# Writing the zero rows of an expert layer's output later, and issuing weight loads behind the first gathers

## The chip, the cores and the metric

The kernel runs on one core of one Trainium2 chip. The metric is the device time of one execution in microseconds (us), lower is better. Three runs of the kernel before gave 581.94, 584.55 and 584.72 us; the median is 584.55 us.

## What is computed

A global filter layer (real FFT along the sequence, product with a complex filter, inverse FFT) feeds an expert layer with a capacity: of the tokens whose largest logit belongs to an expert, only the 80 with the largest gate weight go through it. All other rows of the output are zero.

```python
X = np.fft.rfft(x, axis=1)                       # x: 8 x 2496 x 256, float32
y = np.fft.irfft(X * (filt_r + 1j * filt_i), n=2496, axis=1).reshape(19968, 256)
logits = y @ w_gate                              # 8 experts
expert_idx = np.argmax(logits, axis=1)
gate_w = softmax(logits)[row, expert_idx]
out = np.zeros((19968, 256), np.float32)
for e in range(8):
    tok_idx = the 80 rows of expert e with the largest gate_w
    out[tok_idx] = gate_w[tok_idx, None] * (np.maximum(y[tok_idx] @ w1[e], 0) @ w2[e])
```

So 19,968 rows of 1 KB are written as zero, and 8 x 80 of them are overwritten by the expert outputs.

## The kernel before

The transform of 2496 = 39 x 64 points is done as two matrix products with tables, one batch element (of 8) after another. A loop of steps k = 10 b + u, ten for each batch element b, interleaves three kinds of TensorE work:

- `stage2(b, u)`, line 347, multiplies two frequency blocks by the table `d_t`; VectorE multiplies by the filter (line 354) and GpSimd combines (lines 359, 361).
- `stage1(b + 1, u)`, line 289, in steps u = 0 to 5, transforms one of six chunks of the next batch element's input `x`; ScalarE copies the product and issues its write to a buffer `d1` in device memory (line 292).
- `turn(b, u)`, line 371, two steps later, turns the filtered spectrum and computes gate terms. For batch elements 3 to 6 the spectrum goes to device memory as `yf` (line 399); for 0, 1, 2 and 7 it stays on the chip.

Transfers of the loop: `load_x` (line 267, tile `x`, three transfers a chunk) reads input three steps ahead; `load_t2` (line 298, tile `t`, ten transfers for a batch element) reads the turned `d1` back in steps 7, 8 and 9. Both are issued by SP in the order of the program: an SP instruction that waits holds up all that follow on SP. Each SP or ScalarE transfer takes one of eight completion semaphores, and where one is taken again the earlier transfer on it is waited for, so some eight transfers are under way at a time.

`put_zeros(n)` (lines 182 to 190) issues the next n of 26 zero writes, each 768 rows (786,432 bytes) from one tile of zeros. It is called with 1 after every third step from k = 11 on (line 546), and with all that are left (`NZ`) at line 816.

After the loop come the last two batch elements' gate terms (lines 409 to 507), the token pick (`pick`, lines 594 to 753: a long chain of small VectorE operations), and `back` (lines 763 to 792) for each batch element: a gather of table rows for the picked tokens by GpSimd (line 772, tile `gt`), transposes (line 781) and products with the spectrum (line 786). `spectrum` (line 796, tile `yb`) reads `yf` back for batch elements 3 to 6; the first two reads are issued ahead of the pick. Then a branch (line 822), not taken here, and the experts: `gather(e)` (line 851, tile `xg`) takes an expert's 80 rows, `layer1` (lines 861 to 874) and `layer2` (lines 882 to 886) compute, `load_weights` (lines 581, 583, tile `w`) reads 2 MB for an expert.

Inside the loop the order is that of the program. Behind it a scheduler orders each engine's instructions, and it may place a transfer that depends on nothing ahead of where it is written.

Of the kernel before, what the change touches and what calls it, by code (L numbers as in the profile page):

```python
# [38 lines left out]
NZ = 26  # L39
# [36 lines left out]
def kernel(  # L76
# [107 lines left out]
    def put_zeros(n):  # L184
        for i in zeros[:n]:
            r = N // NZ
            m = r * C // 128
            nc.sync.dma_start(
                out=out[i * r:i * r + r, :].rearrange("r d -> (r d)").rearrange(
                    "(p k m) -> p k m", p=128, m=512),  # L190
                in_=zero_t[:].unsqueeze(1).to_broadcast([128, m // 512, 512]))
        del zeros[:n]
# [4 lines left out]
    with ExitStack() as fctx:  # L197
# [315 lines left out]
        with tc.manual_schedule():  # L513
            load_tables(0)
            load_tables(1)
            for ch in range(5):
                load_x(0, ch)
            load_d(0)
            load_x(0, 5)
            for t in range(B, B + NX):  # L520
                nc.gpsimd.dma_start(out=y_sel[128 * t:128 * t + 128, :], in_=zero_t[:, 0:C])
            xs = [(b, ch) for b in range(1, B) for ch in range(len(CHUNKS))]

            def ahead(g):
                if g < NS // SG:
                    if g:
                        load_d(g)
                    for k in range(2):
                        load_filter(k, g)

            def step(k):
                b, u = divmod(k, NU)
                if b < B:
                    stage2(b, u)
                if b + 1 < B and u < len(CHUNKS):

                    while xs and xs[0] <= divmod(6 * b + 6 + u + min(k, 3), 6):
                        load_x(*xs.pop(0))
                    stage1(b + 1, u)
                if k >= LATE:  # L540
                    turn(*divmod(k - LATE, NU))
                if b + 1 < B and u in (7, 8, 9):
                    for g in ((0, 1), (2, 3), (4,))[u - 7]:
                        load_t2(b + 1, g)
                if k % 3 == 2 and k >= NU:
                    put_zeros(1)
                if b % 2 == 0 and 0 < b < B and u in (2, 3, 5, 6, 8):
                    logits(b // 2 - 1, (2, 3, 5, 6, 8).index(u))
                if b % 2 == 1 and 1 < b < B and u in (1, 2, 4, 5, 7, 9):
                    gating(b // 2 - 1, (1, 2, 4, 5, 7, 9).index(u))  # L550

            ahead(0)
            ahead(1)
            for ch in range(len(CHUNKS)):
                stage1_near(ch)
            for g in range(NS // SG):
                turn_near(g)
                for k in range(2):
                    turn_filter(k, g)
                ahead(g + 2)  # L560
                step(2 * g)
                step(2 * g + 1)
                if g == NS // SG - 1:
                    load_tables(2)
            for k in range(NU, B * NU + LATE):
                step(k)
            for part in range(5):
                logits(B // 2 - 1, part)
            for part in range(NG):
                gating(B // 2 - 1, part)  # L570
# [185 lines left out]
    def gather_gates():  # L756
        nc.gpsimd.memset(gate[:], 0.0)
        for e in range(E):
            nc.gpsimd.indirect_dma_start(
                out=gate[:, e:e + 1], out_offset=None, in_=gates_dram[:, :],  # L760
                in_offset=bass.IndirectOffsetOnAxis(ap=idxs[:, e:e + 1], axis=0),
                bounds_check=N - 1, oob_is_err=False)

    def back(mp, mps, nm, loads, put, idx, start=True, stop=True, acc=None, pad=False):


        gt = mp.tile([128, NS * 128], F32, name=f"gt_{nm}", tag="gt")
        kw = {}
        if pad:
            nc.gpsimd.memset(gt[:], 0.0)  # L770
            kw = dict(bounds_check=S - 1, oob_is_err=False)
        nc.gpsimd.indirect_dma_start(
            out=gt[:], out_offset=None, in_=rows[:, :],
            in_offset=bass.IndirectOffsetOnAxis(ap=idx, axis=0), **kw)
        yb = loads()
        wt = mp.tile([128, NS, 128], F32, name=f"wt_{nm}", tag="wt")
        for g in range(NS // SG):
            ps = mps.tile([128, SG, 128], F32, name=f"pw_{nm}_{g}", tag="pt")
            for i in range(SG):
                s = SG * g + i  # L780
                nc.tensor.transpose(ps[:, i, :], gt[:, 128 * s:128 * s + 128], ident[:])  # L781
            copy = nc.vector.tensor_copy if g % 2 == 0 else nc.scalar.copy
            copy(out=wt[:, SG * g:SG * g + SG, :], in_=ps[:])  # L783
        po = mps.tile([128, C], F32, name=f"pr_{nm}", tag="po") if acc is None else acc
        for s in range(NS):
            nc.tensor.matmul(po[:], lhsT=wt[:, s, :], rhs=yb[s // SG][:, s % SG, :],  # L786
                             start=(start and s == 0), stop=(stop and s == NS - 1))
        if put is not None:
            yr = mp.tile([128, C], F32, name=f"yr_{nm}", tag="yr")
            nc.vector.tensor_copy(out=yr[:], in_=po[:])  # L790
            nc.sync.dma_start(out=y_sel[put:put + 128, :], in_=yr[:])
        return po

    def spectrum(pool, tag, b, nm):
        yb = pool.tile([128, NS, C], F32, name=f"yb_{nm}", tag=tag)
        nc.sync.dma_start(out=yb, in_=yf[b])
        return [yb[:, SG * g:SG * g + SG, :] for g in range(NS // SG)]

    away = [b for b in range(B) if b not in KEEP]
    with (  # L800
        tc.tile_pool(name="mp", bufs=2) as mp,
        tc.tile_pool(name="mps", bufs=2, space=PSUM) as mps,
    ):
        yb = {b: spectrum(keep_b, "kb", b, f"{b}") for b in away[:2]}
        with (
            tc.tile_pool(name="pick", bufs=1) as sp,
            tc.tile_pool(name="pkps", bufs=1, space=PSUM) as pp,
        ):
            pick(sp, pp)
        for i, b in enumerate(away):  # L810
            back(mp, mps, f"{b}", lambda: yb.pop(b), 128 * b, idxb[:, b:b + 1])
            if i + 2 < len(away):
                yb[away[i + 2]] = spectrum(keep_b, "kb", away[i + 2], f"{away[i + 2]}")
            else:
                load_weights(i + 2 - len(away))
        put_zeros(NZ)
        for b in KEEP:
            back(mp, mps, f"{b}", lambda: yk[b], 128 * b, idxb[:, b:b + 1])
        gather_gates()

    n_bad = nc.values_load(bad[0:1, 0:1], min_val=0, max_val=1 << 20)
# [56 lines left out]
    def layer2(e):  # L878
# [10 lines left out]
            in_=ys[:], in_offset=None, bounds_check=N - 1, oob_is_err=False,  # L889
        )  # L890

    for e in range(2, 5):
        load_weights(e)
    gather(0)
    gather(1)
    layer1(0)
    for e in range(E):
        if e + 2 < E:
# [392 lines left out]
```

## Time and profile before

| | |
|---|---|
| median of 3 runs | 584.55 us |
| profiled execution | 586.85 us |
| its span on the core | 585.0 us |
| PE (TensorE matmul) busy | 464.3 us (79%) |
| DVE, ACT, POOL busy | 222.2, 127.0, 174.5 us |
| moved by DMA | 135.92 MB, 232 GB/s over the span |
| waits of line 289 for `x`, whole span | 26.2 us |
| waits of line 347 for `t`, whole span | 17.7 us |

PE is TensorE's matmuls, PEld its weight loads, DVE is VectorE, ACT ScalarE, POOL GpSimd, SP SyncE. The clock column gives the TensorE clock that was granted, as a share of full speed: 0.50 is 1.2 GHz and 1.00 is 2.4 GHz. The DMA share is the mean busy share of the core's 16 DMA engines; the profile shows stretches a little over 1.00. The profiled execution's 586.85 us is its span and 1.85 us around it.

### The profile page before, as it was taken

To read this page: it belongs to the slowest core of one execution; us is meant where nothing else is said; L and a number is where in the kernel's file an instruction comes from. 1 tells how busy PE (TensorE), PEld (TensorE's weight loads), DVE (VectorE), ACT (ScalarE), POOL (GpSimd) and SP (SyncE) were. 2 spreads that over 40 slices of the span, in tenths; PEclk is the share of its full clock that TensorE was granted. 3 is DMA by queue.
4 is the path that set the end of the run, shared out by engine and by line. 5 is a ranking of instruction groups with operands and counts; after the bars stand their busy time and mean duration, and the time that the engine had idled before them with its cause. 6 is when DMAs were issued, how large, how long until landed. Compare 5 with 4: busy or idle time off the path is not lost. (4 is left out here: it accounts for less than half of the span.)

```text
span 585.0 us, 7928 instructions
## 1 busy us (share of the span) xinstructions
PE 464.3 (79%) x2867; PEld 380.5 (65%) x2867; DVE 222.2 (38%) x500; ACT 127.0 (22%) x236; POOL 174.5 (30%) x253
## 2 busy tenths in 40 slices
PE   6498979789877989894997887114999999199994
PEld 6466948578656758574676874013888888098882
DVE  5334724335537316553325853781112211000110
ACT  2124323323332323431331221000001100000110
POOL 5012423414327324445334560115200100202111
PEclk9879988899979879997989995555999999659997
DMA  7968997978989989999998921704798620676700
GB/s 215 222 183 230 252 321 254 271 258 267 291 281 303 344 302 281 359 292 299 332 310 235 354 78 57 302 1 180 259 360 275 247 99 12 222 250 214 257 12 11
DMA packets 63625, 135.92 MB, mean 232 GB/s; under 512 B 6652, under 2 KB 35324, under 8 KB 61916
## 3 DMA queue, kind: packets, MB, share of 16 engines
q1 hardware_dynamic: 51956, 93.46, 51.9%
q0 software_dynamic: 5824, 22.90, 10.5%
q10 hardware_dynamic: 5800, 18.98, 9.9%
q8 instruction: 25, 0.41, 0.3%
q14 instruction: 20, 0.16, 0.1%
HBM read 83.16 MB, written 52.16 MB: 231 GB/s over the span
## 5 line engine op out<-in xcount | busy, mean ns | idle before, releaser
L354 DVE TENSOR_TENSOR p<-pb,ft 128x512 f32<-128x512 f32 x160 | 102.7, 683 | 50.0 <-PE pb L347 38.5
L359 POOL TENSOR_TENSOR yt<-p,p 128x256 f32<-128x256 f32 x80 | 59.7, 746 | 188.4 <-DVE p L354 143.9
L371 PEld LDWEIGHTS py<-gi,yt 128*128 128x128 f32 x640 | 88.1, 200 | 33.3 <-issue 22.4
L289 PE MATMUL pa<-x,wf_t 117*120 117x512 f32 x154 | 86.5, 686 | 26.2 <-DMA x<-in_x_dram 26.2
L347 PE MATMUL pb<-d_t,t 128*128 128x128 f32 x640 | 89.8, 285 | 17.7 <-DMA t<-d 17.7
L371 PE MATMUL py<-gi,yt 128*128 128x136 f32 x640 | 92.8, 290 | 8.6 <-POOL yt L361 8.6
L347 PEld LDWEIGHTS pb<-d_t,t 128*128 128x128 f32 x640 | 81.7, 199 | 21.2 <-issue 20.8
L291 ACT COPY t<-pa 120x512 f32<-120x512 f32 x77 | 44.5, 586 | 122.1 <-PE pa L289 99.1
L289 PEld LDWEIGHTS pa<-x,wf_t 117*120 117x120 f32 x154 | 28.6, 208 | 49.3 <-issue 44.8
L394 DVE TENSOR_REDUCE z<-py 128x16 f32<-128x32 f32 x80 | 15.2, 189 | 116.9 <-ACT ysp L391 66.3
L361 POOL TENSOR_TENSOR yt<-p,p 128x256 f32<-128x256 f32 x80 | 59.2, 740 | 0.0
L868 PEld LDWEIGHTS ph<-xs,w 128*128 128x128 f32 x256 | 36.1, 227 | 0.6
L786 PE MATMUL pr<-yb,wt 128*128 128x256 f32 x160 | 36.3, 382 | 0.0
L868 PE MATMUL ph<-xs,w 128*128 128x80 f32 x256 | 36.0, 311 | 0.0
L786 PE MATMUL pr<-yk,wt 128*128 128x256 f32 x160 | 35.9, 379 | 0.0
L391 ACT COPY ysp<-py 128x512 f32<-128x512 f32 x40 | 23.2, 585 | 49.5 <-PE py L371 42.6
L781 PE MATMUL pw<-ident,gt 128*128 128x128 f32 x160 | 24.3, 296 | 11.1 <-DMA gt<-rows_tbl,idxb 8.3
L783 ACT COPY wt<-pw 128x512 f32<-128x512 f32 x16 | 9.4, 586 | 107.4 <-PE pw L781 107.4
L786 PEld LDWEIGHTS pr<-yb,wt 128*128 128x128 f32 x160 | 30.1, 192 | 3.7
L391 ACT COPY yk<-py 128x512 f32<-128x512 f32 x40 | 23.3, 585 | 41.7 <-PE py L371 40.0
L786 PEld LDWEIGHTS pr<-yk,wt 128*128 128x128 f32 x160 | 29.8, 190 | 3.7
L882 PE MATMUL po<-w,hT 128*80 128x256 f32 x128 | 31.0, 392 | 0.0
(157 smaller groups left out, 377.9 us busy)
## 6 DMA issues: line engine op xcount, KB each, us to landing
out_dram<-zero_t SPq DMA_DIRECT2D x26, 768.0 KB
x<-in_x_dram SPq DMA_DIRECT2D x120, 156.0 KB
t<-d SPq DMA_DIRECT2D x70, 256.0 KB
d<-t ACTq DMA_DIRECT2D x35, 480.0 KB
w<-in_moe_w_dram SPq DMA_DIRECT2D x16, 1024.0 KB
yf<-ysp POOLq DMA_DIRECT2D x20, 512.0 KB, 7.1
yb<-yf SPq DMA_DIRECT2D x4, 2560.0 KB
x<-in_x_dram SPq DMA_DIRECT2D x23, 78.0 KB
```

What stands on the lines that cost most here:

```text
L289: nc.tensor.matmul(out=ps[0:NM1], lhsT=wf_t, rhs=xt[0:NP1, 2 * i:2 * i + 2, :], start=True, stop=True)
L291: nc.scalar.copy(out=t1[:, 2 * i:2 * i + 2, :], in_=ps[0:NM1])
L347: nc.tensor.matmul(out=ps[:, i, cb], rhs=d_t[:, s, :], start=True, stop=True, lhsT=st["t2", b, s // SG][:, s % SG, 128 * cb:128 * cb + 128])
L354: nc.vector.tensor_tensor(out=pt, in0=ps[:].rearrange("p s c r q -> p (s c) r q"), in1=f.unsqueeze(2).to_broadcast([128, 2 * NDB, 2, NQ]), ...
L359: nc.gpsimd.tensor_tensor(out=yt[:, :, 0, :], in0=pr[0][:, :, 0, :], in1=pr[1][:, :, 1, :], op=AL.subtract)
L361: nc.gpsimd.tensor_tensor(out=yt[:, :, 1, :], in0=pr[0][:, :, 1, :], in1=pr[1][:, :, 0, :], op=AL.add)
L371: nc.tensor.matmul(out=ps[:, i, 136 * cb:136 * cb + 136], rhs=gi[:, cb, :], lhsT=yt[:, 2 * i + cb].rearrange("p r q -> p (r q)"), start=Tr ...
L391: nc.scalar.copy(out=ys[:, m:m + 2, :].rearrange("p i (k c) -> p i k c", k=NDB), in_=ps[:, :, 0:288].rearrange("p i (k c) -> p i k c", k=N ...
L781: nc.tensor.transpose(ps[:, i, :], gt[:, 128 * s:128 * s + 128], ident[:])
L786: nc.tensor.matmul(po[:], lhsT=wt[:, s, :], rhs=yb[s // SG][:, s % SG, :], start=(start and s == 0), stop=(stop and s == NS - 1))
L868: nc.tensor.matmul(ph[:, fc // 4, fc % 4, 0:cap], lhsT=w1s[e][:, k, 128 * fc:128 * fc + 128], rhs=xs[:, k, :], start=(k == 0), stop=(k == ...
L882: nc.tensor.matmul(po[0:cap, :], lhsT=hT[:, fc, :], rhs=w2s[e][:, fc, :], start=(fc == 0), stop=(fc == NFC - 1))
```

## The change

The call in the loop is gone. Ten zero writes are written in the program ahead of the first two spectrum reads, six behind them, and then 4, 4 and 2 behind the `back` of batch elements 0, 1 and 2. At the experts, the loads of the weights 2 to 4 are written behind `gather(0)` and `gather(1)`.

```diff
@@ step(k), in the loop
-                if k % 3 == 2 and k >= NU:
-                    put_zeros(1)
@@ behind the loop
+        put_zeros(10)
         yb = {b: spectrum(keep_b, "kb", b, f"{b}") for b in away[:2]}
+        put_zeros(6)
...
-        put_zeros(NZ)
         for b in KEEP:
             back(mp, mps, f"{b}", lambda: yk[b], 128 * b, idxb[:, b:b + 1])
+            put_zeros(4 if b < 2 else 2)
         gather_gates()
@@ experts
+    gather(0)
+    gather(1)
     for e in range(2, 5):
         load_weights(e)
-    gather(0)
-    gather(1)
     layer1(0)
```

On SP, in the loop around the reads `t` of batch element 3, the kernel before has these rows (`x` and `t` are the loads, `out_dram<-zero_t` a zero write; the number in `t_3_0` is the batch element, then the group):

```order
L267 DMA x_0_1177<-in_x_dram 39x1024 x3
L188 DMA out_dram<-zero_t 384x1x512
L267 DMA x_1_1221<-in_x_dram 39x1024 x3
L267 DMA x_2_1252<-in_x_dram 39x1024 x3
L188 DMA out_dram<-zero_t 384x1x512
L298 DMA t_3_0_1333<-d_3_1073 64x4x256 x2
L298 DMA t_3_1_1336<-d_3_1073 64x4x256 x2
L298 DMA t_3_2_1358<-d_3_1073 64x4x256 x2
L298 DMA t_3_3_1361<-d_3_1073 64x4x256 x2
L298 DMA t_3_4_1394<-d_3_1073 64x4x256 x2
L188 DMA out_dram<-zero_t 384x1x512
L267 DMA x_3_1410<-in_x_dram 39x1024 x3
```

And the changed kernel at the same place:

```order
L267 DMA x_0_1173<-in_x_dram 39x1024 x3
L267 DMA x_1_1216<-in_x_dram 39x1024 x3
L267 DMA x_2_1247<-in_x_dram 39x1024 x3
L298 DMA t_3_0_1327<-d_3_1070 64x4x256 x2
L298 DMA t_3_1_1330<-d_3_1070 64x4x256 x2
L298 DMA t_3_2_1352<-d_3_1070 64x4x256 x2
L298 DMA t_3_3_1355<-d_3_1070 64x4x256 x2
L298 DMA t_3_4_1388<-d_3_1070 64x4x256 x2
L267 DMA x_3_1403<-in_x_dram 39x1024 x3
```

Seventeen single zero writes have left SP's queue between the loads of batch elements 1 and 7 in this way.

On SP from the last input chunk of the loop to the fourth spectrum read, before (`yb` is a spectrum read, `y_sel` the result rows of a `back`):

```order
L267 DMA x_5_2465<-in_x_dram 1x512
L188 DMA out_dram<-zero_t 384x1x512 x4
L298 DMA t_7_0_2659<-d_7_2404 64x4x256 x2
...
L298 DMA t_7_3_2688<-d_7_2404 64x4x256 x2
L188 DMA out_dram<-zero_t 384x1x512
L298 DMA t_7_4_2723<-d_7_2404 64x4x256 x2
L188 DMA out_dram<-zero_t 384x1x512 x4
L796 DMA yb_3096<-yf_122 128x5120
L796 DMA yb_3098<-yf_123 128x5120
L821 TENSOR_LOAD bad
```

And in the changed kernel:

```order
L267 DMA x_5_2448<-in_x_dram 1x512
L188 DMA out_dram<-zero_t 384x1x512 x4
L298 DMA t_7_0_2640<-d_7_2387 64x4x256 x2
...
L298 DMA t_7_4_2703<-d_7_2387 64x4x256 x2
L188 DMA out_dram<-zero_t 384x1x512 x8
L794 DMA yb_3082<-yf_122 128x5120
L794 DMA yb_3084<-yf_123 128x5120
L188 DMA out_dram<-zero_t 384x1x512 x13
L794 DMA yb_3297<-yf_124 128x5120
L789 DMA y_sel<-yr_3294 128x256
L188 DMA out_dram<-zero_t 384x1x512
```

Four zero writes stand ahead of the last batch element's `t` reads in both; eight now follow them where five stood, thirteen follow the first two spectrum reads, and one stands behind the third.

On SP behind the branch the kernel before loads the weights in these rows:

```order
L822 UNCONDITIONAL_BRANCH x2
L581 DMA w_7094<-in_moe_w_dram 128x2x1024
L583 DMA w_7094<-in_moe_w_dram 128x8x256
L581 DMA w_7097<-in_moe_w_dram 128x2x1024
L583 DMA w_7097<-in_moe_w_dram 128x8x256
```

And the changed kernel in these:

```order
L822 UNCONDITIONAL_BRANCH x2
L579 DMA w_7098<-in_moe_w_dram 128x2x1024
L581 DMA w_7098<-in_moe_w_dram 128x8x256
L579 DMA w_7101<-in_moe_w_dram 128x2x1024
L581 DMA w_7101<-in_moe_w_dram 128x8x256
```

Only line numbers and names differ. The gathers are issued by GpSimd, another queue, whose rows behind the branch are also the same in both kernels, and so are the semaphores that the loads and the gathers wait for.

## Rows read from the trace of the kernel before

**Rows 1.** Windows: span, busy us of PE, PEld, DVE, ACT, POOL, clock, DMA share, GB/s.

```profile
85.00:295.00 210.00, 179.33 (x1086) 139.58 (x1087) 93.30 (x191) 67.12 (x118) 85.59 (x125) 0.91 0.94 295
345.00:403.00 58.00, 20.19 (x133) 14.79 (x132) 31.22 (x107) 4.53 (x9) 11.10 (x16) 0.55 0.31 120
```

**Rows 2.** Groups of PE's instructions from 85 to 295 us: busy, mean | idle before.

```profile
L289 PE MATMUL pa<-x,wf_t 117*120 117x512 f32 x114 | 65.3, 698 | 17.0 <-DMA x<-in_x_dram 17.0
...
L347 PE MATMUL pb<-d_t,t 128*128 128x128 f32 x400 | 55.6, 284 | 13.7 <-DMA t<-d 13.7
```

**Rows 3.** Windows around the first wait for x in the loop.

```profile
81.00:84.00 3.00, 0.00 (x0) 0.00 (x0) 0.19 (x2) 1.66 (x3) 0.00 (x0) 1.00 0.88 299
...
87.00:90.00 3.00, 3.00 (x10) 1.95 (x9) 0.00 (x0) 1.09 (x2) 0.00 (x0) 0.50 0.93 328
```

**Rows 4.** Timeline of PE: start, us, instruction, count, idle before and what ended it.

```profile
73.35 1.88 PE L289 MATMUL pa<-x,wf_t 117*120 117x512 f32 x4
...
84.85 3.74 PE L289 MATMUL pa<-x,wf_t 117*120 117x512 f32 x4 [4.26 <-DMA x<-in_x_dram]
...
188.65 1.13 PE L347 MATMUL pb<-d_t,t 128*128 128x128 f32 x8 [2.25 <-DMA t<-d]
...
207.66 3.74 PE L289 MATMUL pa<-x,wf_t 117*120 117x512 f32 x4 [3.34 <-DMA x<-in_x_dram]
```

**Rows 5.** Timeline of SP's queue: zero writes and the loads beside them.

```profile
84.44 1.08 SPq L188 DMA_DIRECT2D out_dram<-zero_t  x1
...
179.91 0.54 SPq L188 DMA_DIRECT2D out_dram<-zero_t  x1
...
188.81 0.62 SPq L188 DMA_DIRECT2D out_dram<-zero_t  x1
...
195.83 9.64 SPq L267 DMA_DIRECT2D x<-in_x_dram  x6
...
278.84 0.57 SPq L188 DMA_DIRECT2D out_dram<-zero_t  x1
...
294.80 4.48 SPq L188 DMA_DIRECT2D out_dram<-zero_t  x4
```

**Rows 6.** The page's list of DMA issues: count, KB each.

```profile
out_dram<-zero_t SPq DMA_DIRECT2D x26, 768.0 KB
...
yb<-yf SPq DMA_DIRECT2D x4, 2560.0 KB
```

**Rows 7.** Issue of the zero writes on SP: ns least, median, most; first and last.

```profile
L188 SPq DMA_DIRECT2D out_dram<-zero_t x26: 539/596/2300, 84.4 to 326.9; - x26
```

**Rows 8.** Windows of the loop's end and of the spectrum reads.

```profile
332.00:336.00 4.00, 3.85 (x34) 3.65 (x33) 3.93 (x10) 1.17 (x2) 2.79 (x4) 1.00 1.04 409
...
340.00:344.00 4.00, 3.11 (x28) 2.92 (x27) 1.93 (x6) 1.45 (x4) 3.85 (x7) 1.00 0.02 5
...
368.00:372.00 4.00, 1.08 (x4) 0.71 (x4) 2.31 (x5) 0.26 (x2) 2.02 (x4) 0.50 0.98 420
...
376.00:380.00 4.00, 0.00 (x0) 0.00 (x0) 3.73 (x13) 0.00 (x0) 0.00 (x0) 0.50 0.03 7
```

**Rows 9.** Timeline: spectrum reads, first table gather, first transposes.

```profile
362.06 0.95 SPq L796 DMA_DIRECT2D yb<-yf  x2
...
396.38 1.06 POOL L772 DMA_INDIRECT gt<-rows_tbl,idxb  x1 [3.21 <-issue]
...
403.15 3.85 PE L781 MATMUL pw<-ident,gt 128*128 128x128 f32 x16 [8.33 <-DMA gt<-rows_tbl,idxb]
```

**Rows 10.** Timeline behind the branch, and the landing time of all xg gathers.

```profile
501.61 0.39 SPq L581 DMA_DIRECT2D w<-in_moe_w_dram  x1
...
502.67 0.91 POOL L851 DMA_INDIRECT xg<-y_sel,idxg  x1 [35.02 <-DVEq L822]
...
510.27 0.50 PE L861 MATMUL px<-ident,xg 80*128 80x80 f32 x2 [12.48 <-DMA w<-in_moe_w_dram]
...
DMA to landing us min/median/max: 6.0/6.7/7.2
```

## The prediction

> **What bounds the kernel now.** I read the windows by stage first. From 85 to 295 us, the part of the loop in which single zero writes are issued, the 16 DMA engines are busy for 0.94 of the time while PE is busy for 179.33 of 210 us at a mean clock of 0.91 [rows 1]. So the transfers are the fuller of the two. The groups of PE's instructions in the same stretch say what PE waits for: 17.0 us for the input `x` and 13.7 us for the turned spectrum `t` [rows 2], 30.7 us together, and no wait for another engine is near that size. The timeline shows single waits: 4.26 us for `x` at 84.85, 2.25 us for `t` at 188.65, 3.34 us for `x` at 207.66 [rows 4]. Each has a second cost. After PE stood still from 81 to 84, the granted clock was 0.50 from 87 to 90 [rows 3], which is 1.2 GHz, and four matmul records of line 289 took 3.74 us where they take 1.88 us at 73.35 [rows 4].
>
> Over the stretch, a mean clock of 0.91 means 18% of the time at half speed: (1 - 0.91) / 0.5. That is 37.8 us, and if PE worked through it, half of it, 18.9 us, is lost. Waits and clock together are an upper bound of what better fed matmuls could give: 30.7 + 18.9 = 49.6 us. PE's own work at full clock, with its other waits, is then 210 - 49.6 = 160.4 us.
>
> Behind the loop, from 345 to 403 us, it is the other way: DMA share 0.31, and VectorE's chain of small operations sets the end [rows 1].
>
> **The change, part by part.** Part one takes zero writes out of the loop. Between 84.44 and 278.84 SP issues 17 single ones; the first and the last are shown, and each is 768 KB, 786,432 bytes [rows 5, 6]. The four issued at 294.80 [rows 5], ahead of the last `t` reads, stay where they are by the order of the changed kernel, so the delay that they cause there stays too; I cost that at nothing.
>
> What is one such write worth to the DMA engines? The window from 332 to 336, which holds mostly zero writes, moved 409 GB/s at a full share [rows 8]: 786,432 bytes / 409 GB/s = 1.92 us. Seventeen are 32.7 us. The stretch had 0.94 x 210 = 197.4 us of DMA work; 164.7 us are left. PE needs 160.4 us. The two become equally full.
>
> The gain of the loop is now bounded from both sides. Before, the stretch took 210 us with 197.4 us of the fuller resource, a factor of 1.064. Were that factor kept, it would take 164.7 x 1.064 = 175 us, a gain of 35 us. The factor should get worse, since two resources that are equally full wait for each other in turn. The low end: if only SP's issue time is won, it is 17 x 0.596 us [rows 7] = 10 us. Two observations place the value between. The wait at 84.85 came with no zero write ahead of it (the first is issued at 84.44), so a part of the waits is made by the loads' own burst: `t` and `x` together. Against that, in the batch element around 200 us the zero writes of 179.91 and 188.81 stand ahead of the `x` load of 195.83 [rows 5], whose data ended the wait at 207.66; 2 x 1.92 = 3.8 us of transfers stand against 2.25 + 3.34 = 5.6 us of waits [rows 4]. Nothing there, two thirds here: I take half of the 49.6 us, 25 us. The stretch then takes 185 us, a factor of 1.12 over 164.7.
>
> Part two is where the writes go. Eight stand behind the last `t` reads where five stood. Three more are 5.8 us. DMA fell to 5 GB/s at 340 to 344 [rows 8], and the spectrum reads start only at 362.06 [rows 9]: 22 us of idle DMA hide them. Without that cover they would delay the spectrum reads by 5.8 us, which have 403.15 - 376 = 27 us to spare: the reads are done at 376, where the rate falls to 7 GB/s [rows 8], and their first use comes after the transposes that start at 403.15 [rows 9]. Cost nothing.
>
> Thirteen stand behind the two spectrum reads, in the token pick. The two reads are 5.24 MB [rows 6], 12.5 us at 420 GB/s; thirteen zero writes are 10.22 MB, 25.0 us at 409 GB/s [rows 8]. From 362.06 this ends at 399.6 us. The first table gather is issued by GpSimd at 396.38 and its data start PE at 403.15 [rows 9]. So 3.2 us of zero writes are still under way, in the latency of the gather for the most part. PE waits on that gather, and everything behind it follows, so what it loses is on the path. The ends: 0 if the overlap falls into the latency. At the loop's 295 GB/s [rows 1] the thirteen need 34.7 us behind the reads' 376, to 410.7; if the gather has to wait for all of that, as much as 410.7 - 399.6 = 11 us. I take 2 us, near the measured rate.
>
> The Trainium skill (DMA: Bandwidth & Descriptors, Where 436 GB/s comes from) states that transfers between device memory and SBUF are held to about 358 GB/s for a core. The windows with 409 and 420 GB/s [rows 8] differ from that, and the measurement decides. By the page, an estimate, the 15.46 MB would end 43.2 us after 362.06, at 405.3, and the gather would meet 8.9 us of them. The same page (Queues, rings and completion order) states that each DMA engine takes turns between queues, so the gather would share the engines and not wait its full turn behind the zero writes. No row here shows two such queues against each other. By both rules the loss would be some 4 us instead of 2, an estimate, and the time 564 us.
>
> Nothing on VectorE's chain waits for a transfer that the change moves. Behind the thirteen on SP stand the third spectrum read, which cannot start before the first `back` ends, and the load of the branch's flag, needed only behind the last `back`. The one zero write behind the third spectrum read is 1.92 us of DMA in a stage that PE fills: nothing.
>
> Part three, weights behind the gathers, moves no instruction: rows and semaphores on SP and GpSimd are the same. SP issues the first weight load at 501.61, GpSimd the first gather at 502.67, and PE starts at 510.27 after a wait of 12.48 us [rows 10]. The gather takes 7.6 us there against a median of 6.7 us [rows 10], so even a true reordering would be worth about 0.9 us. I take 0, ends 0 and 0.9.
>
> The sum: 25 - 2 + 0 = 23 us. The profiled execution took 586.85 us, 585.0 us of it span, and would become 563.85 us. It stands 2.3 us above the median of the three runs, 584.55 us, by which the change is measured: 584.55 - 23 = 561.6, so 562 us.
>
> **The rivals.** First, the loop is bound by the burst and the order of the loads, not by bytes. For it: the wait at 84.85 with no zero write ahead, and SP issues loads in order, so `x` stands behind ten `t` reads. Against it: the share of 0.94 over the whole stretch. Then only SP's 10 us are won, less 2 us: 584.55 - 8 = 577 us.
>
> Second, nearly all waits go, and the clock stays up: the full 35 us, no loss at the gather, 584.55 - 35 = 549.6, so 550 us. For it: the zero writes account for two thirds of the waits near 200 us, and removing a wait also removes the slow stretch behind it. Against it: PE's 160.4 us and DMA's 164.7 us leave no slack.
>
> Third, on the other side: the thirteen zero writes hold the first gather until they have drained. Its place is 396 to 411 us, its price the 11 us above. It decides only from the point where the loop wins less than that. With the loop at 5 us (half of SP's issue time), the time is 584.55 + 11 - 5 = 591 us. Against it: the gather is issued on another queue than the writes.
>
> A fourth, that the change does not do what it says, is true of the weights, at 0 us, and partly of the zero writes: twelve of the 26 are placed ahead of the pick, in the loop's last batch element. That is in the sum.
>
> **How the numbers follow.** My forecast, 562 us with its own range of 554 to 572, has a chance of 0.63; the burst (577) 0.16; the full gain (550) 0.15; the held gather (591) 0.06. The range of 546 to 578 reaches over the second rival and most of the first, and leaves out the third and the tails. About 0.5% (2.9 us, 581.6 to 587.5) is what a measurement of this kernel can tell from no change. Of the first rival's 0.16, 0.06 lie there; faster: 0.63 + 0.15 + 0.10 = 0.88, same 0.06, slower 0.06.
>
> **What would show it.** In the loop, PE's waits for `x` and `t` over the same batch elements should fall from 30.7 us to about half, the mean clock rise above 0.94, and the last single-write stretch end some 25 us earlier. The distance from the spectrum reads to the first transposes should stay at 41 us (403.15 - 362.06) plus about 2, with the DMA share near 1 for some 37 us of it. From the branch to the end nothing should change. The forecast is wrong if those waits stay near 30 us, or if the transposes start 5 us or more later against the reads.

## The result, and the profile after

The changed kernel took 557.29 us, median of four runs (554.01 to 562.65), beside 584.63 us for the kernel before (581.94 to 587.22): a ratio of 0.9514, 95% interval 0.9425 to 0.9603. Measured twice more, beside the experiments, it gave 560.76 us at 0.9655 (0.9608 to 0.9703) and 558.84 us at 0.9627 (0.9575 to 0.9679). So the change is worth 20 to 28 us. The profiled executions of three experiments below (e4, e7, e9) were disturbed ones and longer than their undisturbed runs; from these three only single distances are used, never a total.

The profiled execution of the changed kernel took 554.01 us, 551.8 us of it span. The span falls into pieces at points that every trace has: first load of a turned spectrum `t`; issue of the two spectrum reads `yb`; issue of the first table gather; first transposes of what it brought; first transposes of the token gather behind the branch (`px`).

| us | before | after |
|---|---|---|
| start to first `t` | 62.38 | 61.11 |
| loop: first `t` to `yb` | 299.68 | 264.90 |
| `yb` to first gather | 34.32 | 34.33 |
| first gather to its transposes | 6.77 | 10.99 |
| transposes to `px` | 107.12 | 105.71 |
| `px` to end | 74.73 | 74.76 |

In this pair of profiles the loop gave 34.8 us, and the first gather took 4.2 us back. Little else moved: the pieces before the loop and behind the transposes are 1.3 and 1.4 us shorter.

Windows of the changed kernel (columns as in [rows 1]):

```profile
85.00:255.00 170.00, 158.21 (x1043) 126.69 (x1042) 91.61 (x187) 64.53 (x114) 81.34 (x120) 0.98 0.88 268
326.00:337.00 11.00, 1.09 (x4) 0.71 (x4) 8.26 (x15) 1.34 (x3) 2.02 (x4) 0.56 0.91 360
337.00:343.00 6.00, 1.02 (x2) 0.10 (x2) 4.58 (x19) 0.00 (x0) 0.00 (x0) 0.50 0.97 337
343.00:369.00 26.00, 2.63 (x39) 2.48 (x39) 14.82 (x62) 0.00 (x0) 9.41 (x11) 0.50 1.05 398
```

The first row answers to the first of [rows 1]: in the loop the clock is 0.98 where it was 0.91, PE is busy for 93% of the time where it was 85%, and the DMA share has fallen from 0.94 to 0.88. The other three answer to [rows 8] and to the idle stretch of [rows 1]: from the spectrum reads to the first transposes the engines are now full nearly all the time.

PE's groups from the first `t` load (61 us) to the last `t` loads (before: the stretch of [rows 2]; after: 62 to 284 us):

```profile
L347 PE MATMUL pb<-d_t,t 128*128 128x128 f32 x495 | 67.0, 279 | 3.1 <-DMA t<-d 3.1
L289 PE MATMUL pa<-x,wf_t 117*120 117x512 f32 x132 | 65.2, 613 | 10.9 <-DMA x<-in_x_dram 10.7 <-issue 0.2
```

The waits for `x` and `t` fell from 17.0 and 13.7 us [rows 2] to 10.7 and 3.1 us, and one matmul of line 289 from a mean of 698 ns to 613 ns: that is the clock.

Timeline of the changed kernel (start, us, engine, instruction, idle before):

```profile
83.43 2.24 PE L289 MATMUL pa<-x,wf_t 117*120 117x512 f32 x4 [3.79 <-DMA x<-in_x_dram]
...
104.03 1.13 PE L347 MATMUL pb<-d_t,t 128*128 128x128 f32 x8 [2.56 <-DMA t<-d]
...
264.51 5.42 SPq L188 DMA_DIRECT2D out_dram<-zero_t  x4
281.86 7.55 SPq L298 DMA_DIRECT2D t<-d  x10
289.46 14.09 SPq L188 DMA_DIRECT2D out_dram<-zero_t  x8
326.01 1.28 SPq L794 DMA_DIRECT2D yb<-yf  x2
327.36 30.64 SPq L188 DMA_DIRECT2D out_dram<-zero_t  x13
...
360.34 1.06 POOL L770 DMA_INDIRECT gt<-rows_tbl,idxb  x1 [3.21 <-issue]
...
371.33 3.85 PE L779 MATMUL pw<-ident,gt 128*128 128x128 f32 x16 [12.55 <-DMA gt<-rows_tbl,idxb]
374.97 0.66 PE L784 MATMUL pr<-yb,wt 128*128 128x256 f32 x2
...
468.85 0.39 SPq L579 DMA_DIRECT2D w<-in_moe_w_dram  x1
...
477.04 0.50 PE L861 MATMUL px<-ident,xg 80*128 80x80 f32 x2 [11.79 <-DMA xg<-y_sel,idxg]
```

The wait at 83.43, the first of the loop, is nearly that of 84.85 in [rows 4]: no zero write stood ahead of it in either kernel. The zero writes stand where the prediction put them: four ahead of the last `t` loads, eight behind, thirteen behind the spectrum reads. The gather's data now end a wait of 12.55 us where it was 8.33 us [rows 9]. From the weight load to `px` it is 8.19 us, before 8.66 us [rows 10].

One row was not foreseen. The issue of the zero writes (ns least, median, most), to be read beside [rows 7]:

```profile
L188 SPq DMA_DIRECT2D out_dram<-zero_t x26: 547/1795/9237, 264.5 to 385.3; - x26
```

Singly, a write left SP in 596 ns. In a row most take about as long as their transfer (1795 ns against 1.92 us), and one, behind the spectrum reads, took 9.24 us, so thirteen hold SP for 30.64 us. Here nothing urgent stood behind them (the third `yb` read left at 384.30 us); in experiment e7 something did.

### The profile page after: what moved, and what is told of

It is laid out like the page before. It is cut to its first block, busy times and chain, and to the rows that moved or that the text cites. A ratio compares the mean times of both kernels' runs of the same rounds, so it can differ in the third digit from the quotient of the medians.

```text
span 551.8 us, 7938 instructions
## 1 busy us (share of the span) xinstructions
PE 446.6 (81%) x2867; PEld 370.6 (67%) x2867; DVE 222.3 (40%) x500; ACT 127.3 (23%) x236; POOL 174.2 (32%) x253
## 5 line engine op out<-in xcount | busy, mean ns | idle before, releaser
L371 PEld LDWEIGHTS py<-gi,yt 128*128 128x128 f32 x640 | 85.3, 194 | 30.1 <-issue 20.0
L371 PE MATMUL py<-gi,yt 128*128 128x136 f32 x640 | 90.5, 285 | 7.9 <-POOL yt L361 7.9
L289 PE MATMUL pa<-x,wf_t 117*120 117x512 f32 x154 | 77.5, 623 | 20.4 <-DMA x<-in_x_dram 20.1
L347 PE MATMUL pb<-d_t,t 128*128 128x128 f32 x640 | 86.6, 279 | 5.5 <-DMA t<-d 5.5
L347 PEld LDWEIGHTS pb<-d_t,t 128*128 128x128 f32 x640 | 78.8, 193 | 9.0 <-issue 5.5
L289 PEld LDWEIGHTS pa<-x,wf_t 117*120 117x120 f32 x154 | 25.8, 188 | 40.0 <-issue 32.2
L779 PE MATMUL pw<-ident,gt 128*128 128x128 f32 x160 | 24.0, 293 | 15.3 <-DMA gt<-rows_tbl,idxb 12.5
L779 PEld LDWEIGHTS pw<-ident,gt 128*128 128x128 f32 x160 | 19.0, 149 | 20.5 <-issue 12.6
```

The costliest lines, as they stand in the source:

```text
L289: nc.tensor.matmul(out=ps[0:NM1], lhsT=wf_t, rhs=xt[0:NP1, 2 * i:2 * i + 2, :], start=True, stop=True)
L347: nc.tensor.matmul(out=ps[:, i, cb], rhs=d_t[:, s, :], start=True, stop=True, lhsT=st["t2", b, s // SG][:, s % SG, 128 * cb:128 * cb + 128])
L371: nc.tensor.matmul(out=ps[:, i, 136 * cb:136 * cb + 136], rhs=gi[:, cb, :], lhsT=yt[:, 2 * i + cb].rearrange("p r q -> p (r q)"), start=Tr ...
```

## The experiments

The main theory: the loop's transfers were short of time, so each zero write taken out gives back about its transfer time, and the weights give nothing. Rival one: the loads' own burst makes the waits, and only SP's slots are won. Rival three: the first gather is held until the writes ahead have drained.

All stretches in us. "Loop" is the first gather's issue less 34.33 us, less the first `t` load; "waits" are PE's for `x` (line 289) and for `t` over the whole span, 26.2 and 17.7 in the profile before; ratios are against the kernel before on the same chip, with 95% interval.

| | loop | gather | transposes to `px` | waits | median | ratio |
|---|---|---|---|---|---|---|
| before | 299.7 | 6.77 | 107.1 | 26.2, 17.7 | 584.63 | |
| changed | 264.9 | 10.99 | 105.7 | 20.1, 5.5 | 557.29 | 0.9514 (0.9425 to 0.9603) |
| e1 | 296.2 | 6.78 | 106.7 | 25.6, 17.5 | 582.86 | 0.9988 (0.9936 to 1.0041) |
| e2 | 272.1 | 6.80 | 106.2 | 22.0, 6.9 | 561.68 | 0.9626 (0.9527 to 0.9725) |
| e3 | 268.9 | 6.75 | 106.2 | 21.7, 3.6 | 556.1 | 0.9503 (0.9407 to 0.9598) |
| e4 | | 6.72 | | | 560.45 | 0.9585 (0.9503 to 0.9666) |
| e5 (changed) | 272.0 | 10.91 | 105.9 | 20.7, 6.4 | 560.76 | 0.9655 (0.9608 to 0.9703) |
| e6 | 282.2 | 6.76 | 106.2 | 23.5, 10.7 | 570.01 | 0.9781 (0.9699 to 0.9863) |
| e7 | | 11.58 | | | 579.43 | 0.995 (0.9912 to 0.9988) |
| e8 | 270.2 | 11.38 | 105.5 | 10.4, 17.4 | 559.19 | 0.9614 (0.9556 to 0.9672) |
| e9 (changed) | | 10.71 | | | 558.84 | 0.9627 (0.9575 to 0.9679) |
| e10 | 264.8 | 6.76 | 113.6 | 18.9, 2.5 | 561.03 | 0.9689 (0.9633 to 0.9745) |
| e11 | 257.4 | 6.76 | 113.0 | 9.6, 10.4 | 555.0 | 0.9572 (0.9512 to 0.9632) |
| e12 | 266.5 | 6.71 | 106.0 | 9.9, 15.9 | 554.4 | 0.9531 (0.9482 to 0.958) |

Two profiles of the same changed kernel differ by 7 us in the loop (264.9 and 272.0; the third, e9, has 271.8, so the first is the low one). A loop difference of a single pair of profiles is read with that in mind. The medians scatter too: two of the changed kernel's own three intervals, 0.9425 to 0.9603 and 0.9608 to 0.9703, do not overlap, so a gap of that size between two kernels measured apart shows nothing. Steadier are the gather (10.7 to 11.0) and the stretch behind it (105.7 to 105.9), which repeat to a few tenths.

**e1: the weights alone.** The kernel before, with the loads of weights 2 to 4 put behind the first gathers:

```diff
-    for e in range(2, 5):
-        load_weights(e)
     gather(0)
     gather(1)
+    for e in range(2, 5):
+        load_weights(e)
```

> The kernel before, with only the weight loads written behind the first two gathers. Main theory (that part moves no instruction): within 0.5% of before, 582 to 587 us, and from the first weight load to the first transposes of the experts 8.7 us as before (501.61 to 510.27). Rival (the gathers get ahead of the weight loads): the transposes start 2 to 5 us sooner, 580 to 582 us.

Measured: no difference beyond 0.6%, 0.9988 with 1 inside the interval. The first weight load left at 498.69 us and `px` began at 506.83, 8.14 us later against 8.66 us [rows 10]. So the change's gain is in the zero writes.

**e2: the same writes, an eighth of their bytes.** The kernel before, its seventeen writes of the loop cut:

```diff
-    def put_zeros(n):
+    def put_zeros(n, part=128):
-            r = N // NZ
+            r = N // NZ * part // 128
...
-                    put_zeros(1)
+                    put_zeros(1, 16 if k < 62 else 128)
```

> The kernel before with the same number of transfers in the same places, but the 17 single zero writes of the loop write 32 KB instead of 768 KB; the rest of those rows is left unwritten. Main theory (the bytes of the zero writes held up the loads): from the first t read of the loop to the first t read of the last batch element about 221 to 225 us, as in the changed kernel (220.8), where before had 252.4; first table gather 6.8 us from issue to the transposes; 549 to 554 us in all. Rival (what holds up the loads is a place in SP's queue and a completion semaphore, whatever the size): about 245 to 252 us there and 577 to 585 us in all.

The page's list of DMA issues of e2:

```profile
out_dram<-zero_t SPq DMA_DIRECT2D x9, 768.0 KB
...
out_dram<-zero_t SPq DMA_DIRECT2D x17, 96.0 KB
```

Each write has 96 KB, an eighth; the 32 KB of the expectation is a slip. SP still issues seventeen instructions in the loop, at the same places, and the loop still falls to 272.1 us, the second value of the changed kernel. So bytes made the loop long and SP's slots did not: rival one's price, 10 us for the slots, falls. The time, 561.68 us, is above what the main theory had expected, because the loop kept more waits than it allowed for. e3 asks why.

**e3: no zero write at all.** The changed kernel without its three calls of put_zeros:

```diff
-        put_zeros(10)
...
-        put_zeros(6)
...
-            put_zeros(4 if b < 2 else 2)
```

> The changed kernel without any zero write; rows that no expert writes are left unwritten. Main theory (the thirteen writes in the pick delay the first gather by about 4 us, the four ahead of the last t reads cost about 5 us): gather to transposes 6.8 us instead of 11.0, first to last t reads about 216 us instead of 220.8, 544 to 550 us in all. Rival (the gather is late for another reason, such as its place beside the gate gathers; the last batch element's t reads are late through the last input loads): 11 us and 221 us stay, 553 to 558 us.

PE's groups of e3 from 85 to 285 us:

```profile
L289 PE MATMUL pa<-x,wf_t 117*120 117x512 f32 x120 | 62.1, 638 | 10.7 <-DMA x<-in_x_dram 10.4 <-issue 0.2
L347 PE MATMUL pb<-d_t,t 128*128 128x128 f32 x424 | 57.2, 278 | 3.6 <-DMA t<-d 3.6
```

Two findings. The gather took 6.75 us, so the 4.2 us there come from the thirteen writes. And 14.0 us of waits stay in a loop that writes no zeros at all, as much as the 13.8 us of the changed kernel: these are not the zero writes' doing. Here rival one was right about a part, and the expected 544 to 550 us were too low: it came to 556.1.

The trace shows one thing that may make these waits besides the loads' burst. SP's own waits from 60 to 285 us, in e3 and then in the changed kernel (us in all, times, longest):

```profile
SPq L267 <- DMA d<-t: 78.1, 22, 8.2
...
SPq L267 <- DMA d<-t: 74.7, 25, 8.1
```

`d<-t` is ScalarE's write of the first stage, which takes its completion semaphores from the same eight as SP's transfers. The loads of `x` stand behind these writes on SP for some 75 us in all. At the loop's first wait for `x`, SP stood for such a write for 4.9 us before, 5.2 us in the changed kernel and 5.1 us in e3, between the second and the third transfer of the chunk that PE waited for. No run separates this from the burst.

The four writes ahead of the last `t` loads cost nothing, or a few us: from the `t` loads of one batch element earlier to the spectrum reads it is 85.4 us in e3 (248.65 to 334.09), 85.5 us in the changed kernel (240.51 to 326.01), but 88.9 us in its second profile, e5 (244.15 to 333.09).

**e6: nine of the seventeen back in the loop.**

```diff
+                if k % 6 == 5 and NU <= k < 62:
+                    put_zeros(1)
```

> The changed kernel with nine of the 17 single zero writes back in the loop, one in every sixth step; four instead of thirteen follow the first two spectrum reads. Main theory (the loads wait for bytes, and the waits shrink with each write that is gone): loop from the first t read to the spectrum reads about 281 us, midway between 299.7 before and 264.9 in the changed kernel; gather to transposes 6.8 us; 564 to 572 us in all. Rival (below some load the writes find room between the loads and cost nothing): loop as in the changed kernel, 265 to 270 us; 551 to 556 us in all.

As expected: the loop stands between the two kernels, 282.2 us, and the median is 570.01 us. With seventeen writes it took 296.2 and 299.7, with none 264.9 to 272.0. From 298.0, the mean of the first two, to 268.5, the mean of the last two, it is 29.5 us, or 1.74 us for each write, against 1.92 us of transfer by [rows 8]. The gather took 6.76 us; only four writes stood behind the spectrum reads.

**e5 and e9: the changed kernel again,** unedited, as the yardstick beside the other experiments.

> The changed kernel once more, beside the three below on one chip. All theories: 554 to 561 us; gather to transposes 11 us, against 6.8 us before.

> The changed kernel a third time, as the measure for the two beside it on the same chip: 554 to 562 us, 0.95 to 0.97 of before; first gather 11 us to the transposes.

Both below 1 by a clear distance, at 0.9655 and 0.9627, near the upper end of the first interval. The gather repeated at 10.91 and 10.71 us.

**e8: `x` one step earlier.** The changed kernel, with each load of `x` issued four steps ahead instead of three:

```diff
-                    while xs and xs[0] <= divmod(6 * b + 6 + u + min(k, 3), 6):
+                    while xs and xs[0] <= divmod(6 * b + 6 + u + min(k, 4), 6):
```

> The changed kernel with the input loaded four steps ahead instead of three, so that one more chunk of x is issued ahead of the ten t reads of a batch element. Theory (the waits for x that are left, 10.7 us, come from x standing behind the ten t reads on SP): these waits fall under 4 us and the loop by 5 to 10 us, 545 to 553 us in all. Rival (the DMA engines are full there in any order): the waits go over to t, loop and time as in the changed kernel, 553 to 561 us.

PE's groups of e8 from 85 to 285 us:

```profile
L289 PE MATMUL pa<-x,wf_t 117*120 117x512 f32 x120 | 60.4, 623 | 1.8 <-ACT t L291 1.7
L347 PE MATMUL pb<-d_t,t 128*128 128x128 f32 x440 | 59.9, 280 | 11.0 <-DMA t<-d 11.0
```

and of e5 in the same window:

```profile
L289 PE MATMUL pa<-x,wf_t 117*120 117x512 f32 x119 | 61.9, 641 | 8.4 <-DMA x<-in_x_dram 7.8 <-ACT yk L391 0.6
L347 PE MATMUL pb<-d_t,t 128*128 128x128 f32 x440 | 58.9, 277 | 2.9 <-DMA t<-d 2.9
```

The waits for `x` are gone in this window, and as much came back as waits for `t`: 10.7 us together in e5, 11.0 us in e8. The loop moved by 1.8 us, within its scatter, and the time, 559.19 us, is the rival's: putting `x` ahead made `t` late. That both come over the same engines in one burst would explain it, but the DMA engines were busy for 0.87 of e5's window and not full on average, and SP's standing for ScalarE's writes is left (75.5 us in e8, 76.7 in e5).

**e7: all 26 writes behind the spectrum reads.** So that they can't be placed earlier, the zero tile is made again at the loop's end from the routing scores times zero:

```diff
-        put_zeros(10)
         yb = {b: spectrum(keep_b, "kb", b, f"{b}") for b in away[:2]}
-        put_zeros(6)
+        nc.vector.tensor_scalar(out=zero_t[:], in0=lg[:, T - 64:T, :].rearrange("p t e -> p (t e)"),
+                                scalar1=0.0, scalar2=None, op0=AL.mult)
+        put_zeros(NZ)
```

> The changed kernel with all 26 zero writes behind the first two spectrum reads: their tile of zeros is computed from the last logits, so none can be issued before the pick (0.7 us on VectorE's chain). 50 us of writes behind the reads, which end some 30 us after the first table gather is issued. Main theory (the gather's queue shares the DMA engines with SP's queue): gather to transposes 10 to 14 us, hardly more than with thirteen; later spectrum reads stand behind the writes on SP, so 556 to 568 us in all. Rival (the gather waits until the writes have drained): 30 us or more from gather to transposes, 575 to 585 us in all.

Timeline of e7:

```profile
338.64 68.38 SPq L188 DMA_DIRECT2D out_dram<-zero_t  x26
...
409.20 1.02 SPq L794 DMA_DIRECT2D yb<-yf  x1
...
369.97 1.06 POOL L770 DMA_INDIRECT gt<-rows_tbl,idxb  x1 [3.21 <-issue]
...
381.55 3.50 PE L779 MATMUL pw<-ident,gt 128*128 128x128 f32 x16 [13.14 <-DMA gt<-rows_tbl,idxb]
...
425.17 1.94 PE L779 MATMUL pw<-ident,gt 128*128 128x128 f32 x8 [12.33 <-DMA gt<-rows_tbl,idxb]
430.03 20.35 PE L784 MATMUL pr<-yb,wt 128*128 128x256 f32 x80 [2.92 <-DMA yb<-yf]
```

Rival three's price falls here. Twice as many writes stand behind the reads, and they keep SP until 407.02 us (338.64 + 68.38), yet the gather's data start PE at 381.55, 11.58 us after its issue, hardly later than with thirteen or fourteen (10.7 to 11.4; e8 has fourteen). So the gather does not wait until all of the writes have drained. Nor does it share the engines with them from its issue on. Packets, MB and share of the 16 engines by queue (q0 is GpSimd's, q1 SP's), first in the kernel before from 398 to 404 us, then in the changed kernel from 360.4 to 366 and from 366 to 372 us, then in e7 from 370 to 376 and from 376 to 382 us:

```profile
q0 software_dynamic: 220, 2.09, 95.9%
...
q1 hardware_dynamic: 1085, 2.14, 104.9%
...
q0 software_dynamic: 215, 2.04, 85.1%
q1 hardware_dynamic: 139, 0.26, 16.3%
...
q1 hardware_dynamic: 1107, 2.19, 103.8%
...
q0 software_dynamic: 202, 1.90, 84.9%
q1 hardware_dynamic: 220, 0.42, 20.4%
```

For 6 us after its issue no packet of the gather's queue ran, in the changed kernel as in e7, and SP's had the engines; in the kernel before, the first ran less than 2 us after the issue (396.38). Then the gather moved nearly as much in 6 us as without company: 2.04 and 1.90 MB beside 2.09. So its loss is a late start of some 4 us, as long with 26 writes as with thirteen. What sets that length is not shown.

The expected time, 556 to 568 us, was missed by far, at 579.43: the expectation names the later spectrum reads that stand behind the writes on SP, and priced them too low. The third left at 409.20, in e5 at 391.20. PE waits for it and for a gather near it at 425 and 430 us, together 15.3 us, and from the transposes to `px` it takes 125.7 us in place of 105.9. PE's rows also stand in another order there (eighty `pr` in a row), as in e10 below; what that adds is not separated.

**e4 and e10: all 26 writes directly behind the last `t` loads,** where the engines were idle in [rows 8]:

```diff
+                if k == 7 * NU:
+                    put_zeros(NZ)
...
-        put_zeros(10)
         yb = {b: spectrum(keep_b, "kb", b, f"{b}") for b in away[:2]}
-        put_zeros(6)
...
-            put_zeros(4 if b < 2 else 2)
```

> The changed kernel with all 26 zero writes issued in the loop at step 70, on SP directly behind the last t reads and ahead of the two spectrum reads; complete. Main theory (26 writes are 50 us at 409 GB/s and the spectrum reads 12.5 us, which ends some 10 us ahead of the first gather): same as without zero writes within 2 us, 544 to 552 us, gather to transposes 6.8 us. Rival (the writes ahead of the spectrum reads make these land after the gather, or delay the last t reads by sharing the engines): transposes or first products wait for the spectrum, 556 to 565 us.

> All 26 zero writes directly behind the last t reads, a second time, now beside the changed kernel on one chip. Theory (it saves the 4.2 us of the first gather, and the 2.4 us wait for t behind the four writes): 3 to 6 us less than the changed kernel of this call, gather to transposes 6.8 us. Rival (what the gather loses is won back behind it, since later work has slack): within 1.5 us of the changed kernel.

The gather is back at 6.72 and 6.76 us, and the total, 560.45 and 561.03 us, is no better than the changed kernel's: the theories of both expectations missed. The stretch behind the gather has grown, from 105.9 to 113.6 us. Timeline of e10:

```profile
369.30 5.19 PE L781 MATMUL pw<-ident,gt 128*128 128x128 f32 x24 [8.32 <-DMA gt<-rows_tbl,idxb]
374.80 2.69 PE L781 MATMUL pw<-ident,gt 128*128 128x128 f32 x16 [0.31 <-DVE wt L783]
381.55 1.94 PE L781 MATMUL pw<-ident,gt 128*128 128x128 f32 x8 [4.06 <-DMA gt<-rows_tbl,idxb]
383.28 19.45 PE L786 MATMUL pr<-yb,wt 128*128 128x256 f32 x80
...
374.29 0.97 POOL L772 DMA_INDIRECT gt<-rows_tbl,idxb  x1 [3.10 <-PE pw L781]
377.76 0.96 POOL L772 DMA_INDIRECT gt<-rows_tbl,idxb  x1 [2.50 <-PE pw L781]
...
404.88 0.97 POOL L772 DMA_INDIRECT gt<-rows_tbl,idxb  x1 [22.37 <-PE pw L781]
```

PE's rows stand in another order. In the changed kernel sixteen transposes are followed by the products `pr` of the first gather. With 26 writes in front of the spectrum reads, the scheduler set the transposes of a second and a third gather first (matmul instructions in PE's order; a trace has two records for each `pr`):

```
changed: pw x16 (gather 1), pr x1, pw x4, pr x19, pw x16 (gather 2), pr x1, ...
e10:     pw x20 (gather 1), pw x20 (gather 2), pw x8 (gather 3), pr x20, pr x20, ...
```

The products start 13.98 us after the first transposes (383.28 - 369.30) and not 3.64 us after them, PE stands for the third gather for 4.06 us, and the fifth gather leaves only at 404.88. The products do not wait for the spectrum, which the rival of e4 expected. e12 tries whether the order costs it or the writes' place.

**e11: e10 with `x` four steps ahead.**

> The same, with the input loaded four steps ahead instead of three. If the DMA engines are full in any order, it is within 2 us of the run above; if the order of x and t costs something, 3 us or more faster.

The median is 555.0 us at 0.9572, on the same chip as e10 with 0.9689; the intervals touch but do not overlap. In the profiles the loop is 7.4 us shorter. So what did nothing in e8 seems to gain here, where no zero write stands ahead of any `t` load. With the scatter of the loop and of the medians this is likely, not shown, and why it should need that is open. The stretch behind the gather kept the bad order: 113.0 us.

**e12: the writes split.** As e11, but with two calls, so that the spectrum reads come earlier in the scheduler's order:

```diff
+                if k == 7 * NU:
+                    put_zeros(18)
...
         yb = {b: spectrum(keep_b, "kb", b, f"{b}") for b in away[:2]}
+        put_zeros(NZ)
```

> The 26 zero writes stand in two places of SP's queue: 18 behind the last t reads, 8 behind the two spectrum reads; none stands ahead of the last t reads, and x is loaded four steps ahead. With this split PE's rows of the later `back`s stand in the order of the changed kernel again (transposes of one gather, then its products), not in that of the version with all 26 behind the last t reads. Theory (the loss of 6 us behind the pick there came from the order of the rows, not from the writes): first gather to first transposes 6.8 us, first transposes to the first weight load 98 us in place of 104.6, the rest as in the version with 26 and x four steps ahead (555.0 median), so 547 to 552 us median. Rival (the loss comes with the writes' place, whatever the rows' order): that stretch stays at 104 to 105 us and the median at 553 to 557. If the eight writes still run beside the first gather, that alone shows 8 to 11 us there.

Timeline of e12:

```profile
266.81 6.09 SPq L188 DMA_DIRECT2D out_dram<-zero_t  x4
290.47 35.22 SPq L188 DMA_DIRECT2D out_dram<-zero_t  x18
329.35 1.66 SPq L796 DMA_DIRECT2D yb<-yf  x2
331.06 16.11 SPq L188 DMA_DIRECT2D out_dram<-zero_t  x4
...
370.35 3.85 PE L781 MATMUL pw<-ident,gt 128*128 128x128 f32 x16 [8.27 <-DMA gt<-rows_tbl,idxb]
374.00 1.06 PE L786 MATMUL pr<-yb,wt 128*128 128x256 f32 x2
...
476.31 0.50 PE L861 MATMUL px<-ident,xg 80*128 80x80 f32 x2 [11.45 <-DMA xg<-y_sel,idxg]
```

The writes came to stand otherwise than the expectation says: four went ahead of the last `t` loads, eighteen behind them, four behind the reads. The theory on the order held: sixteen transposes and then products again, the stretch to `px` at 106.0 us, and the gather at 6.71 us. The rival, that the writes behind the last `t` loads cost it whatever the order, falls for the eighteen that still stand there. The median, 554.4 us, is above the 547 to 552 expected, because the loop took 266.5 us and not 257.4. Of these 9.1 us, 4.5 lie ahead of the last two groups of `t` loads, and 4.6 from there to the loop's end: 7.1 between the two groups (241.25 to 283.20 here, 237.56 to 272.42 in e11), the period with the four writes, of which 2.5 come back behind the second. It is the fastest median of all, with a ratio of 0.9531 (0.9482 to 0.958); it was not run beside the changed kernel, two of whose three intervals overlap with it, and whose first ratio, 0.9514, is lower. That it beats the changed kernel is not shown.

## Why the prediction was right, and where it was off

**What bounds the loop: right.** Transfers were the fuller resource. Taking away bytes (e2), half of the writes (e6) or all of them (e3) shortened the loop nearly in proportion, and keeping the instructions while taking the bytes did as much as taking both.

**The loop's gain: right in size.** I took 25 us, half of the waits and the lost clock. In the first pair of profiles it is 34.8 us; with e5 and the mean of the two loops with seventeen writes (298.0), 26.0 us. The medians say the same: 27.3 us net in the first measurement, 580.59 x (1 - 0.9655) = 20.0 us in the second and 580.52 x (1 - 0.9627) = 21.7 us in the third, and with the gather's 4.2 us put back 31.5, 24.2 and 25.9. That half of the waits would stay was right too: 13.8 of 30.7 us. Like the wait at 84.85 [rows 4], which had no zero write ahead, they do not come from the zero writes: the same 14 us are there without any. I put them down to the loads' burst and in part to two equally full resources; no run separates either from SP's standing for ScalarE's writes. The half was a choice between two observations, so that it came this close is partly luck; and in the first measurement the loop gave 6.5 us more than I took and the gather took 2.2 us more, two errors that partly cancel.

**The loop's clock: right.** 0.98 against a forecast of above 0.94; over the whole stretch from the first to the last `t` loads it was 0.92 before, 0.98 in the changed kernel and 0.96 in e5.

**The eight writes behind the last `t` loads: right,** nothing. The first gather follows the reads by 34.33 us in both kernels.

**The first gather: the term was mis-sized, and by another mechanism.** I took 2 us and it was 4.2 (3.9 to 4.6 in the four profiles with thirteen or fourteen writes there). Two things were off. The transfers were under way for longer: the reads took until 376 in [rows 8], and my sum let the writes begin at 374.6 by their full rate; in the changed kernel there is a dip between reads and writes besides, 337 GB/s from 337 to 343 us. And I costed the latency of the gather as cover, while the gather's packets started some 4 us later than alone, as the rows by queue at e7 show. Once started they were hardly slowed. The bound of 11 us stood for a gather that waits until the writes have drained, and e7 excludes that: with twice as many writes behind the reads it lost 4.8 us, while the last of them left SP only 25.5 us after its data had arrived (407.02 - 381.55).

The Trainium skill (DMA: Bandwidth & Descriptors, Queues, rings and completion order) says that each DMA engine takes turns between queues. e7 agrees from 376 us on, where 202 packets of the gather's queue ran beside 220 of SP's in 6 us, but not in the 6 us before, in which only SP's ran. The prediction's estimate from the page, some 4 us, came out right in number, by luck: the loss is the late start and not the shared turns, and its other part, a rate of some 358 GB/s (Where 436 GB/s comes from), does not hold here: the writes ran at 409 GB/s in the window from 350 to 352 us.

**The weights: right,** 0 (e1).

**The rivals.** The burst, at 577 us, is wrong as the whole story and may be the reason for what is left. The full gain, 550 us, was not reached by any version; e11 and e12 came nearest, by moves that the change does not make. The held gather, 591 us, is wrong by e7 in its price and in waiting for the last write; that the gather is held at first, for some 4 us, is what the rows show.

**What is open.** What sets the last 14 us of waits when no zero write is left: the DMA share of e3 was 0.85 from 85 to 285 us, so the engines were not full on average, moving `x` only moved the wait (e8), and SP stood for ScalarE's writes for some 75 us. Open is also what sets the gather's late start, and whether four writes ahead of the last `t` loads cost anything; up to the loop's end, e3 against the two profiles of the changed kernel says 0.1 and 3.5 us, e11 against e12 4.6 us. A version with e11's loop and e12's order behind it was not run.

## What to carry to other kernels

Where the DMA engines are the fuller resource of a stage, price a transfer that could run elsewhere at its bytes over the measured rate, and expect about that back, not the issue slot. Before moving it, list what stands behind it on the queue that issues it, and what it will share the engines with at the new place: here a gather beside a row of large writes started some 4 us late, with twenty-six writes as with thirteen. And compare the scheduler's order far behind the edit too, since the place of a few writes turned round the order of the matmuls 80 us later and ate the gain.

## What the runs showed of the hardware

- A table gather on GpSimd's queue beside zero writes on SP's took 10.7 to 11.6 us in place of 6.7 to 6.8 us, with thirteen writes or with twenty-six. No packet of its queue ran in the first 6 us (alone, the first ran within 2 us); then it moved 1.90 to 2.04 MB in 6 us, alone 2.09 MB.
- SP issued single zero writes in 596 ns, and in a row one per 1.9 to 2.6 us (18 in 35.22 us in e12; 26 in 68.38 us in e7, beside the spectrum reads and gathers): a row of large writes holds the issuing engine for about as long as they take to transfer.
- Executions of the same kernel lay within about 1% of each other on either side (554.01 to 562.65 us, 558.97 to 562.98 us), and the 7.1 us between the two profiled spans (551.8 and 558.9) are in the loop (264.9 and 272.0).
